# Order of the first feed-forward chunk in a fused attention and SwiGLU kernel

## The chip, the cores and the metric

The kernel runs on one core of a Trainium2 chip. The metric is the device time of one execution in microseconds (us), given as the median of five runs. One more view of the kernel is a profile of one execution, in which every instruction of every engine has a start and a length. The engines are named as the profile names them: PE is TensorE's matmul, PEld its weight load, DVE is VectorE, ACT is ScalarE, POOL is GpSimd and SP is SyncE.

## The reference, cut to what matters

Eight batches of eight heads, 576 positions, 64 numbers per head; 32 memory slots. The result of the attention is a matrix of 4608 rows and 512 columns, which goes through a gated feed-forward layer:

```python
a = softmax(phi, axis=2)                       # over the sequence
k_m = einsum('bhsm,bhsd->bhmd', a, k)
v_m = einsum('bhsm,bhsd->bhmd', a, v)
attn = softmax(scale * q @ k_m.T)              # over the 32 memory slots
x = (attn @ v_m)                               # heads side by side: 512 columns
g = x @ w_gate
out = (g * sigmoid(g) * (x @ w_val)) @ w_out   # 512 -> 1536 -> 512
```

## The kernel before, in words

The kernel never forms x. For each batch it multiplies the small matrix v_m (256 rows in all: 8 heads by 32 slots) with the gate and value weights; the products are called U. Gate and value of the layer are then the attention weights A times U. Both are cut into chunks of 512 of the 1536 columns (`NCH` is 3), and a chunk into two halves of 256.

A round of U (`u_round`, line 453) is a set of matmuls `p_u` on TensorE (line 465) into PSUM banks, and then one copy per bank into the SBUF tile `t_U`. Each round for one weight and one half is eight matmuls of 256 columns into two banks, each for half of the heads. A string tells who makes the copies, one letter a bank: "a" is ACT (line 487), "v" is DVE (line 491). In batches 0 and 1 the copy also multiplies by the reciprocal of the softmax's sum. Gate weights are `which` 0, value weights 1. `u_half(b, which, c, half, evac)` is a round of one half of chunk `c`; with `which` (0, 1) it puts gate and value side by side into the same two banks, so that there are 16 matmuls and two copies of 512 columns. `u_item(b, c)` is gate and value of a whole chunk, with four copies.

After it come the slots. A slot is one block of 128 hidden columns by 288 positions; a batch has 24, eight a chunk, and slots 0 to 3 of a chunk use its first half. `gv_gate(b, s)` (line 517) makes two matmuls `p_g` (A times U of the gate, line 508) and a silu on ACT (line 525), and puts the rest on the list `pend`: two matmuls `p_v` with the value half of U and a product on DVE (line 531) into `t_h`. `flush_mul(n)` carries out the first n of the list. `gv_slot` is `gv_gate` and then what was pending before it, so that p_v and the product run one slot behind.

All is ordered by hand: the program's order is the order on each engine's queue, and an engine waits where its next instruction's data are not there. Every matmul group takes the next of eight PSUM banks in turn, in the order of their release in the program (`bank` and `done`, lines 75 to 84). A group therefore waits for the reader of the bank that was taken eight groups earlier.

The weights come by DMA, issued on POOL's queue (`load_w`, line 128). For chunk 0 they come in halves, in the order gate half 0, value half 0, gate half 1, value half 1, after k, q and v of batches 0 and 1; then chunks 1 and 2 whole, then w_out and the inputs of the next batches.

Before the stretch that is changed, attention of batches 0 and 1 is done: `v_direct(1)` makes v_m of batch 1, with its four DVE copies to `t_kT`, and `norm(1, 1)` (line 445) is the last normalization, a DVE product that follows an Exp on ACT (line 421). Softmax uses ACT's table of Ln and Exp; silu needs another table, loaded by `preload_act_table_set`. `warm` (line 868) is matmuls of no result that keep TensorE occupied.

After the stretch, from chunk 1 on, rounds and slots of both batches alternate to the end of chunk 2; then come the output products (line 720) and batches 2 to 7.

Of the kernel before, what the change touches and what calls it, by code (L numbers as in the profile page):

```python
# [14 lines left out]
def kernel(  # L15
# [427 lines left out]
    def norm(b, g):  # L443
        a = att.tile([128, 2, HALF], BF16, tag=f"A{g}", name="t_A")
        nc.vector.tensor_tensor(out=a, in0=es.pop((b, g)), in1=lzs.pop((b, g)), op=ALU.mult)  # L445
        atts[b, g] = a
# [6 lines left out]
    def u_round(b, parts, evac):  # L453


        banks = []
        for which, c, halves in parts:
            w0, w1, h0, h1 = which[0], which[-1] + 1, halves[0], halves[-1] + 1
            n = (h1 - h0) * HC
            p = [bank([128, CH], FP32, f"p_u{g}") for g in range(NG)]  # L460
            for w in which:
                o = (w - w0) * n
                for i in range(NP):
                    for g in range(NG):
                        nc.tensor.matmul(  # L465
                            p[g][32 * i:32 * i + 32, o:o + n],
                            lhsT=kTs[b][64 * g:64 * g + 64, 2, 32 * i:32 * i + 32],
                            rhs=w_part(w, c, i, g, halves),
                            start=True,
                            stop=True,  # L470
                            tile_position=(64 * g, 32 * i),
                        )
            for g in range(NG):
                if (b, c, g) not in Us:
                    u_buffer(b, c, f"U{c}")
                if len(which) == 1:
                    dst = Us[b, c, g][:, h0:h1, w0]
                else:
                    dst = Us[b, c, g][:, h0]
                src = p[g][:, 0:(w1 - w0) * n].rearrange("p (a f) -> p a f", f=HC)  # L480
                banks.append((dst, src, p[g], rSs[b][:, g:g + 1] if b in scaled else None))
        for (t, p, home, r), e in zip(banks, evac):
            if e == "a":
                if r is None:
                    nc.scalar.copy(out=t, in_=p)  # L485
                else:
                    nc.scalar.activation(out=t, in_=p, func=AF.Copy, scale=r)  # L487
            elif r is None:
                nc.vector.tensor_copy(out=t, in_=p)  # L489
            else:  # L490
                nc.vector.tensor_scalar(out=t, in0=p, scalar1=r, scalar2=None, op0=ALU.mult)
            done(home)
# [5 lines left out]
    def flush_mul(n=None):  # L498
        for _ in range(len(pend) if n is None else n):
            pend.pop(0)()  # L500
# [16 lines left out]
    def gv_gate(b, s):  # L517

        jf, r = s // 2, s % 2
        c, o = jf // 4, jf % 4  # L520
        if o == 0 and r == 0:
            hts[b, c] = hpool.tile([128, 4, S], BF16, tag=f"h{c}", name="t_h")
        gate = gv_half(b, s, 0)
        sg = work.tile([128, HALF], BF16, tag="sg", bufs=8, name="t_sg")
        nc.scalar.activation(out=sg, in_=gate[:, 0:HALF], func=AF.Silu)  # L525
        done(gate)
        dst = hts[b, c][:, o, r * HALF:(r + 1) * HALF]

        def mul():
            val = gv_half(b, s, 1)  # L530
            nc.vector.tensor_tensor(out=dst, in0=sg, in1=val[:, 0:HALF], op=ALU.mult)  # L531
            done(val)
            if o == 3 and r == 1:
                chunk_done(b, c)

        pend.append(mul)
# [288 lines left out]
    def u_item(b, c, evac="avav"):  # L825

        return lambda: u_round(b, (((0,), c, (0, 1)), ((1,), c, (0, 1))), evac)

    def u_half(b, which, c, half, evac):

        return lambda: u_round(b, ((which, c, (half,)),), evac)
# [9 lines left out]
    def run(items):  # L841
        for x in items:
            x()
# [13 lines left out]
    def gv_slots(b):  # L857
        return [lambda s=s: gv_slot(b, s) for s in range(2 * NJF)]
# [84 lines left out]


    g0, g1 = gv_slots(0), gv_slots(1)
    run([u_half(0, (0,), 0, 0, "av")])
    nc.scalar.preload_act_table_set("silu_and_others")
    norm(1, 1)
    run([u_half(1, (0,), 0, 0, "vv")])
    for s in range(4):  # L950
        gv_gate(0, s)
    run([u_half(0, (1,), 0, 0, "vv"), u_half(1, (1,), 0, 0, "aa")])
    for s in range(2):
        gv_gate(1, s)
    flush_mul(3)
    run([u_half(0, (0, 1), 0, 1, "va"), u_half(1, (0, 1), 0, 1, "av")])
    flush_mul(2)
    run(g1[2:4] + g0[4:8] + g1[4:5])
    for c in range(1, NCH):
        s = 8 * c  # L960
        run([u_item(0, c)] + g1[s - 3:s] + g0[s:s + 5])
        run([u_item(1, c)] + g0[s + 5:s + 8] + g1[s:s + 5])
    run(g1[-3:])
    flush_mul()
# [146 lines left out]
```

The softmax here doesn't subtract the row's maximum and nothing guards it: scores larger than these inputs give would overflow.

## Time and profile before

| | us |
|---|---|
| Median of five runs | 234.18 |
| Lowest and highest | 234.13 and 234.78 |
| The profiled execution, its own time | 234.78 |
| Span of the profile (first to last instruction) | 233.0 |
| End of the last Exp of the softmax of batches 0 and 1 (ACT) | 24.94 |
| End of the last copy to t_kT (DVE) | 25.89 |
| First round of U starts on TensorE | 25.93 |
| u_item(0, 1) starts | 34.86 |
| u_item(1, 1), u_item(0, 2), u_item(1, 2) start | 39.44, 44.03, 48.61 |
| First output product starts | 54.81 |

All times in the profile are counted from the start of the span. The profiled execution is one of the five, and the slowest of them. The next section shows lines of the profile. A line of the timeline gives start, length, engine, source line, operation, what is written and what is read, and how many instructions are merged into it; in brackets stands the idle time before it and what ended it. The chain of waits is read in order of time: at each step it names the work that the next step had to wait for.

### The profile page before, as it was taken

How to read it: one execution, taken by the hardware profiler on the slowest of the kernel's cores; microseconds unless marked ns; L12 is line 12 of the kernel's file. 1: busy time of each engine (PE TensorE's matmuls, PEld its weight loads, DVE VectorE, ACT ScalarE, POOL GpSimd, SP SyncE). 2: the span in 40 equal slices, each digit the busy share in tenths (PEclk: the TensorE clock that was granted, in tenths of full speed). 3: DMA queues.
4: the chain of work that ended last, by engine and by line, in shares of the span. 5: the costliest groups of instructions: out<-in, count | busy, mean ns of one | idle time of the engine just before them, and what ended most of it. 6: DMA issues, size and time to landing. Idle time of an engine off the chain costs nothing.

```text
span 233.0 us, 7208 instructions
## 1 busy us (share of the span) xinstructions
PE 222.6 (96%) x2825; PEld 169.6 (73%) x2825; DVE 186.3 (80%) x426; ACT 171.2 (73%) x364; POOL 140.6 (60%) x190
## 2 busy tenths in 40 slices
PE   7977899999999999999999999999999999999993
PEld 2544466778887777877788777887788778878882
DVE  4245799999966799989997758998999899977732
ACT  2777798988447989968896658987898789677310
POOL 8422426998099049765977688553945394029291
PEclk9999999999999999999999999999999999999999
DMA  6999999999995992999199994996022702202125
GB/s 210 209 211 206 199 207 207 227 239 268 205 247 129 265 253 47 224 207 188 52 219 197 182 177 90 252 238 109 3 90 92 125 0 94 85 7 90 24 92 159
DMA packets 36674, 36.84 MB, mean 158 GB/s; under 512 B 14624, under 2 KB 31008, under 8 KB 36640
## 3 DMA queue, kind: packets, MB, share of 16 engines
q0 software_dynamic: 16272, 22.42, 52.1%
q1 hardware_dynamic: 19600, 13.18, 23.3%
q10 hardware_dynamic: 768, 0.79, 1.1%
q8 instruction: 22, 0.36, 0.6%
q14 instruction: 12, 0.10, 0.1%
HBM read 42.47 MB, written 9.44 MB: 223 GB/s over the span
## 4 chain that ended last, share of the span: by engine, by line
PE 88%; DMA 7%; POOL 1%; ACT 1%; issue 1%; DVE 1%; POOLq 0%
PE p_g L508 21%; PE p_os L720 21%; PE p_v L508 20%; PE p_oc L720 10%; DMA t_kv<-in_v_dram 7%; PE p_u L465 5%; PE p_oa L720 5%; PE p_kv L230 2%; PE p_g L389 1%; POOL t_kv L99 1%; PE p_mT L318 1%; PE p_warm L868 1%; PE p_q L376 0%; POOL t_q L108 0%; DVE t_kT L332 0%
## 5 line engine op out<-in xcount | busy, mean ns | idle before, releaser
L531 DVE TENSOR_TENSOR t_h<-t_sg,p_v 128x288 bf16<-128x288 bf16 x192 | 81.5, 452 | 14.0 <-PE p_v L508 7.8
L508 PEld LDWEIGHTS <-t_U 128*128 128x128 bf16 x768 | 73.6, 98 | 22.3 <-issue 3.3
L525 ACT ACTIVATE t_sg<-p_g 128x288 bf16<-128x288 f32 x192 | 73.9, 423 | 17.8 <-PE p_g L508 11.5
L508 PE MATMUL p_g<-t_A,t_U 128*128 128x288 bf16 x384 | 77.1, 286 | 0.5 <-ACT t_U L487 0.5
L508 PE MATMUL p_v<-t_A,t_U 128*128 128x288 bf16 x384 | 76.9, 286 | 0.0
L720 PEld LDWEIGHTS <-t_S 128*128 128x128 bf16 x384 | 37.5, 98 | 4.6 <-issue 0.2
L596 POOL TENSOR_TENSOR t_S<-t_h 128x512 bf16<-128x512 bf16 x17 | 19.7, 1156 | 34.3 <-DVE t_h L531 32.2
L720 PEld LDWEIGHTS <-t_h 128*128 128x128 bf16 x288 | 27.1, 98 | 8.6 <-issue 5.0
L485 ACT CAST t_U<-p_u 128x512 bf16<-128x512 f32 x51 | 27.0, 607 | 6.6 <-PE p_u L465 6.6
L720 PE MATMUL p_os<-t_T,t_S 128*128 128x256 bf16 x192 | 23.7, 273 | 0.0
L553 POOL TENSOR_TENSOR t_S<-t_S,t_h 128x512 bf16<-128x512 bf16 x17 | 19.6, 1155 | 1.3
L553 POOL TENSOR_TENSOR t_S<-t_h,t_S 128x512 bf16<-128x512 bf16 x16 | 18.4, 1153 | 0.0
L553 POOL TENSOR_TENSOR t_S<-t_h 128x512 bf16<-128x512 bf16 x16 | 18.4, 1151 | 0.0
L465 PE MATMUL p_u<-W,t_kT 64*32 64x512 bf16 (+1 forms) x416 | 15.8, 364 | 0.6 <-DVE t_kT L332 0.6
L489 DVE CAST t_U<-p_u 128x512 bf16<-128x512 f32 x21 | 13.6, 684 | 1.9 <-PE p_u L465 1.9
L720 PE MATMUL p_os<-t_T,t_h 128*128 128x256 bf16 x96 | 14.8, 273 | 0.0
L868 PE MATMUL p_warm<-bones 128*128 128x512 bf16 x44 | 12.5, 422 | 1.7 <-DVE bones L890 1.7
L445 DVE TENSOR_TENSOR t_A<-t_E,t_lz 128x576 bf16<-128x576 bf16 x16 | 11.4, 740 | 0.7 <-ACT t_lz L421 0.7
L720 PE MATMUL p_oc<-t_T,t_S 128*128 128x256 bf16 x96 | 12.0, 273 | 0.0
L720 PE MATMUL p_oa<-WO,t_h 128*128 128x256 bf16 x96 | 11.8, 273 | 0.0
L720 PE MATMUL p_oc<-WO,t_S 128*128 128x256 bf16 x96 | 11.8, 272 | 0.1
L720 PE MATMUL p_os<-WO,t_h 128*128 128x256 bf16 x96 | 11.8, 273 | 0.0
(106 smaller groups left out, 308.9 us busy)
## 6 DMA issues: line engine op xcount, KB each, us to landing
out_dram<-t_o SPq DMA_DIRECT2D x11, 512.0 KB, 3.0
t_kv<-in_k_dram POOLq DMA_DIRECT2D x8, 576.0 KB, 10.7
t_q<-in_q_dram POOLq DMA_DIRECT2D x8, 576.0 KB, 9.0
t_kv<-in_v_dram POOLq DMA_DIRECT2D x8, 576.0 KB, 15.4
t_phi<-in_phi_dram POOLq DMA_DIRECT2D x6, 576.0 KB, 8.6
out_dram<-t_o SPq DMA_DIRECT2D x10, 256.0 KB, 3.5
WO<-in_moe_w_out_dram POOLq DMA_DIRECT2D x3, 512.0 KB, 19.2
W<-in_moe_w_gate_dram POOLq DMA_DIRECT2D x2, 512.0 KB, 16.4
```

The source lines that it names most:

```text
L230: nc.tensor.matmul(p[g][32 * i:32 * i + 32, 0:n], lhsT=phi_of(b, g, j, i), rhs=kvs[b][64 * g:64 * g + 64, w0:w1, i, j * D:(j + 1) * D], st ...
L445: nc.vector.tensor_tensor(out=a, in0=es.pop((b, g)), in1=lzs.pop((b, g)), op=ALU.mult)
L465: nc.tensor.matmul(p[g][32 * i:32 * i + 32, o:o + n], lhsT=kTs[b][64 * g:64 * g + 64, 2, 32 * i:32 * i + 32], rhs=w_part(w, c, i, g, halve ...
L485: nc.scalar.copy(out=t, in_=p)
L489: nc.vector.tensor_copy(out=t, in_=p)
L508: nc.tensor.matmul(p[:, 0:HALF], lhsT=Us[b, c, g][:, o // 2, which, 128 * (o % 2):128 * (o % 2 + 1)], rhs=atts[b, g][:, r], start=(g == 0) ...
L525: nc.scalar.activation(out=sg, in_=gate[:, 0:HALF], func=AF.Silu)
L531: nc.vector.tensor_tensor(out=dst, in0=sg, in1=val[:, 0:HALF], op=ALU.mult)
L553: eng.tensor_tensor(out=out, in0=x, in1=y, op=ALU.subtract)
L596: eng.tensor_tensor(out=t[:, 0], in0=A21, in1=A22, op=ALU.add)
L720: nc.tensor.matmul(mine[home][:, u], lhsT=lhs(c, m, u), rhs=rhs(c, m), start=fresh and u == 0, stop=(k == 5), skip_group_check=u == 1 or n ...
L868: nc.tensor.matmul(p[:, 0:128 * a], lhsT=bones, rhs=x.to_broadcast([128, a, 128]) if a > 1 else bones, start=True, stop=True,)
```

## The change

It reorders the first chunk of batches 0 and 1. The load of silu's table moves ahead of the first round. The gate half of batch 0, then its value half, then gate and value of batch 1 (side by side, two wide copies) follow one another before any slot; formerly the value halves of both came after the first four slots of batch 0. Copies that were all DVE's or all ACT's are shared by the two. Pending products are flushed in another rhythm: two after the first four slots, then one after each slot of batch 1, and none is left over after the second half's rounds. The second half's copies for batch 1 are both ACT's. One slot more of batch 1 (`g1[4:6]`) stands before `u_item(0, 1)`, and one fewer after it.

```diff
     g0, g1 = gv_slots(0), gv_slots(1)
-    run([u_half(0, (0,), 0, 0, "av")])
     nc.scalar.preload_act_table_set("silu_and_others")
+    run([u_half(0, (0,), 0, 0, "va")])
     norm(1, 1)
-    run([u_half(1, (0,), 0, 0, "vv")])
+    run([u_half(0, (1,), 0, 0, "va"), u_half(1, (0, 1), 0, 0, "av")])
     for s in range(4):
         gv_gate(0, s)
-    run([u_half(0, (1,), 0, 0, "vv"), u_half(1, (1,), 0, 0, "aa")])
+    flush_mul(2)
     for s in range(2):
         gv_gate(1, s)
-    flush_mul(3)
-    run([u_half(0, (0, 1), 0, 1, "va"), u_half(1, (0, 1), 0, 1, "av")])
+        flush_mul(1)
+    run([u_half(0, (0, 1), 0, 1, "va"), u_half(1, (0, 1), 0, 1, "aa")])
     flush_mul(2)
-    run(g1[2:4] + g0[4:8] + g1[4:5])
+    run(g1[2:4] + g0[4:8] + g1[4:6])
     for c in range(1, NCH):
         s = 8 * c
-        run([u_item(0, c)] + g1[s - 3:s] + g0[s:s + 5])
+        run([u_item(0, c)] + g1[s - (2 if c == 1 else 3):s] + g0[s:s + 5])
         run([u_item(1, c)] + g0[s + 5:s + 8] + g1[s:s + 5])
```

## The prediction

> **What bounds the kernel now.** I read the page from the top, then the chain of waits, then the timeline of the stretch that the diff touches. Shares first:
>
> ```profile
> PE 222.6 (96%) x2825; PEld 169.6 (73%) x2825; DVE 186.3 (80%) x426; ACT 171.2 (73%) x364; POOL 140.6 (60%) x190
> ...
> PEclk9999999999999999999999999999999999999999
> ...
> PE 88%; DMA 7%; POOL 1%; ACT 1%; issue 1%; DVE 1%; POOLq 0%
> ```
>
> TensorE holds 88% of the chain at its full clock, so the kernel is bound by TensorE, and only what shortens TensorE's own queue counts. The 7% of DMA lie before 21.2 us, where the inputs arrive. The diff works between 25.9 and 35 us. There the chain of waits reads (start, length, what; x9 means nine instructions):
>
> ```profile
> 25.96 0.37 PE p_u L465 x9
> 26.33 0.47 ACT t_U L487
> ...
> 26.85 1.16 PE p_g L508 x8
> 28.01 0.32 PE p_u L465 x9
> ...
> 28.35 0.30 PE p_u L465 x7
> 28.65 0.63 PE p_g L508 x4
> 29.28 0.85 PE p_v L508 x6
> 30.13 0.78 PE p_u L465 x32
> 30.91 0.60 PE p_v L508 x4
> 31.50 0.24 PE p_g L508 x2
> ```
>
> The reader should see that TensorE is on the chain throughout but not dense. From 31.5 us on, each pair of p_g or p_v matmuls takes 0.245 us, that is 0.1224 each. Before that, one ACT copy stands in the chain, four p_g matmuls take 0.63 in place of 0.49, six p_v take 0.85 in place of 0.73, and a round of sixteen p_u is cut in two at 28.35. The timeline says what the other engines did meanwhile:
>
> ```profile
> 26.82 1.28 ACT L947 ACT_TABLE_LOAD   x1
> ...
> 27.42 1.76 DVE L491 TENSOR_SCALAR t_U<-p_u,t_rS 128x256 bf16<-128x256 f32 x4
> ...
> 28.11 1.32 ACT L525 ACTIVATE t_sg<-p_g 128x288 bf16<-128x288 f32 x4
> 28.35 0.11 PEld L465 LDWEIGHTS <-t_kT 64*32 64x32 bf16 x6 [0.29 <-issue]
> ...
> 30.50 0.14 PEld L465 LDWEIGHTS <-t_kT 64*32 64x32 bf16 x14 [0.21 <-issue]
> 30.58 1.33 ACT L487 ACTIVATE t_U<-p_u,t_rS 128x512 bf16<-128x512 f32 x2
> ```
>
> ACT loads its table for 1.28 us in the middle of this, so DVE has to make four copies in a row. "issue" names no releaser, but the order of the banks does: there are eight, used in turn, so a group of matmuls needs the reader of the bank eight places earlier to be done. At 28.35 that is the second of the four DVE copies (27.42 + 2 x 0.44 = 28.30), at 30.50 the first silu of batch 1. Last, the weights. The DMA issues, each with its time from issue to landing, of a window around 6.7 us:
>
> ```profile
> W<-in_moe_w_gate_dram POOLq DMA_DIRECT2D x1, 256.0 KB, 19.8
> W<-in_moe_w_val_dram POOLq DMA_DIRECT2D x1, 256.0 KB, 20.1
> ```
>
> POOL issued them at 6.01 and 6.74 (timeline), so the first half of the gate weights landed at 25.81 and that of the value weights at 26.84. Nothing waits for the latter now: its round starts at 27.94.
>
> **What the Trainium skill says.** "ScalarE: Activation LUTs", section "What ACT_TABLE_LOAD costs", gives 1283 ns for the load and 1380 ns of drain. The trace agrees on the load (1.28) and shows no drain: the silu starts at 28.11, 0.01 after it. I take 1.28. "TensorE: Matmul & The Clock Gate", section "Why this matters for your kernels", warns of idle gaps over some 3 us, after which the clock falls. The longest gap here is 1.28 us, before 18.29, with the clock full; the gap I expect below is shorter. "DMA: Bandwidth & Descriptors", section "Two DMAs through the same engine are not ordered", says that the completion semaphore is what tells that data has landed: a value round may not start on the strength of the gate half's landing. Its first matmul carries such a wait.
>
> **The change part by part.** The matmuls, the copied elements and the queues of POOL and SP stay as they are. Of the copies, eight narrow (256 columns) and four wide (512) become four narrow and six wide, otherwise shared between ACT and DVE; TensorE's queue is reordered.
>
> *Table load.* It moves to directly behind the last Exp of the normalization, which ends at 24.94, so it runs to 26.22. The first p_u is ready at 26.32. It is covered, with 0.1 us to spare. Without that cover it would cost up to 1.28.
>
> *First gate round and its two copies.* The engines change places; both took 0.47 to 0.48. Nothing.
>
> *Rounds in a row.* Now TensorE has 8 gate, 8 value (batch 0), then 16 (batch 1) p_u matmuls before any p_g. What goes:
> - the wait of the first p_g for the ACT copy, 26.33 to 26.85: 0.52;
> - the bank wait at 28.35: 0.29, as batch 1's round no longer reuses banks of copies just queued on DVE (it takes banks that were read before 25);
> - p_v waiting for the last of the four DVE copies (27.42 + 1.76 = 29.18): 0.63 - 0.49 = 0.14;
> - the bank wait at 30.50: 0.21. The silus of batch 1 now come before the wide copies are wanted: by my count they end at about 29.9 and 30.3, and their banks are next used after 30.5;
> - two changes between p_u and p_g/p_v fewer (five become three). One costs about 0.12: the six p_v above, 0.85 - 0.73. Together 0.24.
>
> Sum of what goes: 1.40.
>
> What comes in its place: the value round stands second in TensorE's queue. The first round starts at 25.93 and has issued its eight by about 26.05 (0.12, an estimate from 16 matmuls of 0.28 that all end within 0.41). Value weights land at 26.84; with 0.04 from landing to start (the v of batch 0: landing 21.13, weight load 21.17) it starts at 26.88. New wait: 0.83. Behind it on TensorE are batch 1's rounds, whose weights are there, and all p_g; behind those, every silu.
>
> From there by hand: 24 p_u and a change of kind bring the first p_g to about 27.35. Ten pairs (four p_g, two p_v, then p_g and p_v twice) of 0.245 bring the second half's rounds to 29.9, against 30.06 before and with one p_v pair more done. The copies keep up: DVE does norm 26.67 to 27.42, a copy of 0.44, then a wide one of 0.70, done at 28.5, and batch 1's first p_g wants it at 28.8. ACT does a narrow copy from 27.2, a wide one, and starts silu at 28.25, 0.14 later than before; the first bank that needs it is wanted at 29.3.
>
> *Second half, "aa".* ACT now has three wide copies of 0.62 to 0.64 in a row from about 30.45, done at 32.35, with the silus of slots 2 and 3 behind them; DVE gets one, and idles. TensorE has seven pairs to do from 30.5, so it wants the last of these banks at 32.2 (gate of slot 5 of batch 0). It waits 0.1; bounds 0 and 0.3, since each start above can be 0.1 off.
>
> *One slot more before the next round.* That round needs value weights that land at 34.53 (issue 18.53, 16.0 to landing); it moves one slot (0.49) back and comes at about 34.9, as before, so there is no wait. The work is the same from the following round on.
>
> Sum: 1.40 - 0.83 - 0.10 = 0.47 us gained, at the hand-over to the next stage (54.7 us before). What could swallow it there is far enough: v of batch 2 lands at 54.35 for matmuls at 59.04, q of batch 2 at 58.54 for 59.77. POOL's sums start behind the same p_v as before and move along. So I carry 0.47 to the end: the profiled execution would take 234.31 instead of 234.78 (its span 232.5 instead of 233.0). The median of the five runs lies 0.60 under that execution, and I take the gain off the median: **233.71, rounded to 233.7**.
>
> **Rivals.**
> - *The value weights are there in time* (233.3). If the landing is not what holds the round, for instance because the runs without a profile fetch faster, the new wait shrinks to that for the first p_g's copies (26.8, about 0.4 of 0.83 saved): gain about 0.85. For it: the profiled execution is the slowest of five by 0.6. Against: batch 1's v, which starts the stretch, comes through the same queue just before, and would be earlier too.
> - *No change* (234.2). ACT's three copies cost the upper 0.3 and the changes of kind bring nothing; or TensorE meets a transfer later, since landings do not move with it. For it: ACT's margin is about nothing. Against: the slacks just given.
> - *Slower* (234.7), by one mechanism: the value weights land later than in this trace. The whole of TensorE's queue stands behind that round, including batch 0's p_g, which needed only gate weights before. Every 0.1 us later costs 0.1; it decides from 27.3 on (26.84 + 0.47) and is slower by over 0.2% from about 27.8. For it: POOL's next issue that waits for this landing ran only at 27.34. Against: that issue also waits for other semaphores, and the others of its kind follow their landings by 0.31.
>
> **How the numbers follow.** Forecast 0.60, weights in time 0.13, no change 0.13, slower 0.14. A measurement of this kernel tells some 0.2%, or 0.47 us, from no change; the forecast sits on that edge. I count 0.7 of its chance beyond it, because where I rounded (the changes of kind, the bank waits) TensorE can as well gain 0.1 more. Faster: 0.42 + 0.13 = 0.55. Same: 0.18 + 0.13 = 0.31. Slower: 0.14. The forecast's own range is 233.45 to 233.95, from the bounds of the ACT wait and 0.15 on the sum of gaps. The range 233.25 to 234.35 takes in the first two rivals and leaves out the last.
>
> **What would show it.** In the profile after: a table load at about 24.95; a TensorE gap of about 0.8 before the second round, with the W DMA as releaser and its start at 26.9; the first p_g at about 27.35; no split at the later rounds; a gap of 0 to 0.3 near 32.3 behind ACT's third copy; the round of chunk 1 at about 34.9 and those after it some 0.5 earlier than 39.4, 44.0 and 48.6. It is wrong if the second round starts before 26.6 or after 27.2, if ACT's copies hold TensorE by over 0.3, or if the lead at 54 us is not there at the end.

## The result, and the profile after

The change makes the kernel a little faster: 233.55 us in the median of 24 runs (233.30 to 234.15), against 234.15 for the kernel before (44 runs). The ratio is 0.9977, 95% interval 0.9972 to 0.9983, that is 0.54 us less (0.40 to 0.66); the two medians alone lie 0.60 apart. The prediction was 233.7, range 233.25 to 234.35. The profiled execution of after took 233.9 us, its span is 232.1.

The page of after, shares of the engines, TensorE's clock, and the chain by engine:

```profile
PE 223.2 (96%) x2825; PEld 170.0 (73%) x2825; DVE 185.3 (80%) x423; ACT 171.6 (74%) x365; POOL 140.6 (61%) x190
...
PEclk9999999999999999999999999999999999999999
...
PE 86%; DMA 9%; POOL 2%; ACT 1%; issue 0%; DVE 0%; POOLq 0%
```

TensorE still bounds the kernel. But DMA's share of the chain has grown from 7 to 9%, and it is another transfer: before, the chain came out of the DMAs at 21.2 us, with v of batch 0; now it comes out at 26.9, with the value weights. A part of this step is only how the first profile of before was read: in a second profile of before the chain comes out of the gate weights, at 25.64, and DMA has 8%. The chain of waits of after, in order of time (start, length, what):

```profile
6.74 20.16 DMA W<-in_moe_w_val_dram
26.91 0.04 issue
26.95 0.52 PE p_u L465 x24
27.47 1.09 PE p_g L508 x8
28.55 0.49 PE p_v L508 x4
29.05 0.24 PE p_g L508 x2
...
30.03 0.56 PE p_u L465 x32
30.59 0.60 PE p_v L508 x4
31.18 0.49 PE p_g L508 x4
...
32.16 0.24 PE p_v L508 x2
32.41 0.35 PE p_g L508 x2
32.76 0.24 PE p_v L508 x2
```

From the landing at 26.90 on, TensorE is dense: p_v and p_g take 0.245 a pair, and the rounds of 24 and 32 are no longer cut. A group that follows a round takes 0.11 more than its pairs (1.09 for eight, 0.60 for four). Beyond that there is one blemish, the pair at 32.41, which stands for 0.35 where 0.245 is due. Who makes what when, from the timeline of after:

```profile
25.27 1.28 ACT L946 ACT_TABLE_LOAD   x1
...
25.78 0.30 PE L465 MATMUL p_u<-W,t_kT 64*32 64x256 bf16 x8
...
26.24 0.48 DVE L491 TENSOR_SCALAR t_U<-p_u,t_rS 128x256 bf16<-128x256 f32 x1
26.57 0.47 ACT L487 ACTIVATE t_U<-p_u,t_rS 128x256 bf16<-128x256 f32 x1
...
26.95 0.52 PE L465 MATMUL p_u<-W,t_kT 64*32 64x256 bf16 x24 [0.86 <-DMA W<-in_moe_w_val_dram]
...
30.46 1.84 ACT L487 ACTIVATE t_U<-p_u,t_rS 128x512 bf16<-128x512 f32 x3 [0.24 <-PE p_u L465]
```

The bracket names the new wait outright. Note the two copies of the first round: DVE starts at 26.24, ACT only at 26.57, right behind the table load, which in this execution ended at 26.55.

For the comparison of runs three times of the timeline do most of the work: the start of the first round, the start of the second (value) round, and the first output product, where the stage ends. Of before and of after there is a second profile, of another execution.

| kernel, one execution each | first round | value round | stage's end | stage's end less first round | stage's end less value round |
|---|---|---|---|---|---|
| before | 25.96 | 27.94 | 54.81 | 28.85 | |
| before, second profile | 25.77 | 27.74 | 54.62 | 28.85 | |
| after | 25.78 | 26.95 | 54.36 | 28.58 | 27.41 |
| after, second profile | 25.88 | 26.65 | 54.06 | 28.18 | 27.41 |

The ends of the stage, in the order of the table, and ahead of the last one the second round of that profile:

```profile
54.81 1.47 PE L720 MATMUL p_os<-WO,t_h 128*128 128x256 bf16 x12
...
54.62 1.47 PE L720 MATMUL p_os<-WO,t_h 128*128 128x256 bf16 x12
...
54.36 1.47 PE L720 MATMUL p_os<-WO,t_h 128*128 128x256 bf16 x12
...
26.65 0.52 PE L465 MATMUL p_u<-W,t_kT 64*32 64x256 bf16 x24 [0.47 <-DMA W<-in_moe_w_val_dram]
...
54.06 1.47 PE L720 MATMUL p_os<-WO,t_h 128*128 128x256 bf16 x12
```

So the kernel before takes 28.85 us from its first round, and the kernel after 27.41 from its second. What the change gains is 28.85 - 27.41 = 1.44, less the distance between the two rounds: 1.17 in the first profile of after, 0.77 in the second. That leaves 0.27 and 0.67. (The ends themselves differ by 0.45 and 0.56, because the first rounds do not start at the same time either.) The distance is set by two DMA landings and differs from execution to execution. Three of the experiments below leave these two rounds as they are in after; in their profiles it is 0.99 (late table load), 1.15 (shared copies) and 0.89 (one slot less). The mean of the five is 0.99, with which the formula gives a gain of 0.45, against 0.54 measured.

The spans differ by 0.9, twice the 0.45 by which the stages' ends differ. The other 0.46 come from a stall in batch 4, told below.

### The profile page after: what moved, and what is told of

The parts are those of the page before. It is cut to its first block, busy times and chain, and to the rows that moved or that the text cites. A ratio compares the mean times of both kernels' runs of the same rounds, so it can differ in the third digit from the quotient of the medians.

```text
span 232.1 us, 7206 instructions
## 1 busy us (share of the span) xinstructions
PE 223.2 (96%) x2825; PEld 170.0 (73%) x2825; DVE 185.3 (80%) x423; ACT 171.6 (74%) x365; POOL 140.6 (61%) x190
## 4 chain that ended last, share of the span: by engine, by line
PE 86%; DMA 9%; POOL 2%; ACT 1%; issue 0%; DVE 0%; POOLq 0%
PE p_g L508 21%; PE p_os L720 21%; PE p_v L508 20%; PE p_oc L720 10%; DMA W<-in_moe_w_val_dram 9%; PE p_oa L720 5%; PE p_u L465 5%; PE p_kv L230 2%; PE p_g L389 1%; POOL t_kv L99 1%; POOL t_kv L103 1%; PE p_q L376 0%; POOL t_q L108 0%; ACT t_qT L330 0%; POOL W L138 0%
## 5 line engine op out<-in xcount | busy, mean ns | idle before, releaser
L465 PE MATMUL p_u<-W,t_kT 64*32 64x512 bf16 (+1 forms) x416 | 15.3, 363 | 0.9 <-DMA W<-in_moe_w_val_dram 0.9
L868 PE MATMUL p_warm<-bones 128*128 128x512 bf16 x44 | 13.9, 459 | 1.7 <-DVE bones L890 1.7
```

What stands on the lines that cost most here:

```text
L465: nc.tensor.matmul(p[g][32 * i:32 * i + 32, o:o + n], lhsT=kTs[b][64 * g:64 * g + 64, 2, 32 * i:32 * i + 32], rhs=w_part(w, c, i, g, halve ...
L868: nc.tensor.matmul(p[:, 0:128 * a], lhsT=bones, rhs=x.to_broadcast([128, a, 128]) if a > 1 else bones, start=True, stop=True,)
```

## The experiments

Ratios are against the kernel before, run beside it.

**The table load put back behind the first round.**

```diff
-    nc.scalar.preload_act_table_set("silu_and_others")
     run([u_half(0, (0,), 0, 0, "va")])
+    nc.scalar.preload_act_table_set("silu_and_others")
     norm(1, 1)
```

> The kernel after with the table load behind the first round's copies again. Theory (the load was covered only because it lies before the first round; behind it, it delays ACT's copies and silus, and TensorE waits for banks and for the value copies): the whole gain goes, 234.1, within 0.15 of the kernel before; in the profile p_v of slot 0 waits for the ACT copy. Rival (the wait for the value weights, 26.1 to 26.9, hides most of the load wherever it is put): at most 0.2 above the kernel after, 233.75.

Measured: 234.17, ratio 0.9998 (0.9990 to 1.0006). The gain is gone, as the theory had it. ACT's lines in the timeline:

```profile
26.21 0.47 ACT L487 ACTIVATE t_U<-p_u,t_rS 128x256 bf16<-128x256 f32 x1 [1.09 <-PE p_u L465]
26.70 1.28 ACT L947 ACT_TABLE_LOAD   x1
28.00 1.05 ACT L487 ACTIVATE t_U<-p_u,t_rS 128x256 bf16<-128x256 f32 x2
28.94 1.91 ACT L525 ACTIVATE t_sg<-p_g 128x288 bf16<-128x288 f32 x6
```

The copy of the value round starts at 28.00 in place of 27.34 and the silus at 28.94 in place of 28.29. From the value round (26.80) to the stage's end (54.69) it takes 27.89, 0.48 more than after. TensorE's lines show where:

```profile
28.25 0.82 PE L508 MATMUL p_v<-t_A,t_U 128*128 128x288 bf16 x4
29.11 0.42 PE L508 MATMUL p_g<-t_A,t_U 128*128 128x288 bf16 x2
...
30.19 0.74 PE L465 MATMUL p_u<-W,t_kT 64*32 64x256 bf16 x32
```

p_v of slot 0 waits for that copy, and the p_g behind it for ACT's next one: from the first p_v to that p_g it is 0.86 (28.25 to 29.11) in place of 0.49 in after (28.39 to 28.88). The round of 32 then takes 0.74 in place of 0.63. Together these are the 0.48; from there on the two profiles run alike. The wait for the value weights does not hide a table load that comes after the first copy, since ACT is needed again as soon as that wait ends.

**The early table load alone, in the kernel before.**

```diff
-    run([u_half(0, (0,), 0, 0, "av")])
     nc.scalar.preload_act_table_set("silu_and_others")
+    run([u_half(0, (0,), 0, 0, "av")])
     norm(1, 1)
```

> The kernel before with nothing but the early table load. Theory (the waits of the kernel before are for copies of the rounds in their old places: the first ACT copy, four DVE copies in a row; only the wait at 30.5 goes, and another bank takes its place): no gain, 234.1, between -0.2 and +0.1 of the kernel before. Rival (the table load in the middle is what cost the time, the order of the rounds is immaterial): the gain of the whole change, 233.55.

Measured: 234.21, ratio 0.9998 (0.9989 to 1.0006): nothing. In its profile the stage takes 28.72 from the first round (25.87 to 54.59), 0.13 less than before. TensorE still waits 0.48 for the first ACT copy and meets the same four DVE copies. The wait at 30.5 is gone, as expected, and pairs further on come late instead (0.28, 0.29 and 0.36 after the one ahead of them at 31.45, 32.47 and 32.83, where 0.245 is due). So neither the early load alone nor the rest of the change without it gives the gain. The rest itself (the rounds in a row, who makes which copy, the rhythm of the flushes) was not taken apart further, but for the "aa" and the extra slot below.

**The second half's copies of batch 1 shared ("av") in the kernel after.**

```diff
-    run([u_half(0, (0, 1), 0, 1, "va"), u_half(1, (0, 1), 0, 1, "aa")])
+    run([u_half(0, (0, 1), 0, 1, "va"), u_half(1, (0, 1), 0, 1, "av")])
```

> The kernel after with the second half's copies for batch 1 shared (one ACT, one DVE) and not both on ACT. Theory (ACT's third copy holds TensorE by 0.1 near 32.3): 0.1 faster than the kernel after, 233.45, and the gap before the gate of slot 5 is gone. Rival (both on ACT frees DVE for the products, and the shared form moves the wait to a product on DVE): 0.1 to 0.3 slower than the kernel after.

Measured: 233.76, ratio 0.9978 (0.9968 to 0.9988), in time not to be told from after's 0.9977. The profile can tell it: from the value round (26.93) to the stage's end (54.23) 27.30, 0.11 less than after's 27.41, and the pair behind 31.98 follows at 32.23, without a gap. At the stage's end the theory's 0.1 is there and the rival's loss is not; the times alone could not exclude a small loss.

**The value weights later.** Both gate halves first, then both value halves; in the kernel after, and as a control in the kernel before.

```diff
-    for half in range(2):
-        for which in range(2):
+    for which in range(2):
+        for half in range(2):
             load_w(which, 0, half)
```

> The kernel after with the weights of chunk 0 fetched in another order: both gate halves, then both value halves, so that the first value half lands third, by about 28.2 in place of 26.9. Theory (TensorE's whole queue stands behind the second round, every 0.1 us later costs 0.1): 1.2 to 1.3 slower than the kernel after, 234.8, with TensorE idle from about 26.1 to 28.2. Rival (the round is not bound by this landing, or the copies and slots behind it have slack that takes up a part): at most 0.6 slower than the kernel after, 234.1.

> The kernel before with the weights of chunk 0 in the order of e4: the first value half lands by about 28.2. Theory (in the kernel before, the value rounds start only at 27.94 and their second half waits for a bank until 28.35 anyway): 0 to 0.3 slower than the kernel before, 234.3, with the clock full, so that the loss of e4 is that of the moved round. Rival (the other order of the weights costs by itself, for instance through the later loads): 1 or more slower, as in e4.

Measured on after: 236.78, but spread: 234.84 and 234.90 in two of seven runs, 236.48 to 237.73 in the others; ratio 1.0092 (1.0060 to 1.0123). The two low runs are the 1.3 of the theory. The others lost about 2 more, which neither theory nor rival had. Each run also has a mean granted clock: 0.996 and 0.997 in the two low ones, as in undisturbed runs of the other kernels, and 0.985 to 0.993 in the five others. The profiled run is one of these five (236.48). The windows of its profile show where the clock was lost (columns: window, length, then busy time and number of instructions of PE, PEld, DVE, ACT and POOL, then the granted clock of TensorE, DMA share, GB/s):

```profile
26.00:27.00 1.00, 0.30 (x8) 0.14 (x9) 0.53 (x2) 0.65 (x2) 0.74 (x1) 1.00 1.45 196
27.00:28.00 1.00, 0.00 (x0) 0.00 (x0) 0.62 (x1) 0.00 (x0) 0.74 (x1) 0.84 1.44 199
28.00:29.00 1.00, 0.87 (x25) 0.44 (x25) 0.39 (x1) 0.36 (x1) 0.63 (x1) 0.50 1.28 207
29.00:30.00 1.00, 1.00 (x5) 0.62 (x6) 0.82 (x2) 1.00 (x3) 0.16 (x2) 0.50 1.24 206
30.00:31.00 1.00, 1.00 (x6) 0.59 (x4) 0.00 (x0) 0.84 (x3) 0.71 (x1) 0.50 1.26 208
31.00:32.00 1.00, 1.00 (x10) 0.78 (x8) 0.53 (x2) 0.53 (x2) 0.00 (x0) 0.95 1.22 203
```

The clock falls to half between 27 and 28 (the mean of 0.84 puts it at about 27.7) and stays there until about 31.1. 3.4 us at half clock are 0.7% of the span, which fits the run's mean of 0.993. On TensorE's timeline of the same profile:

```profile
26.11 0.30 PE L465 MATMUL p_u<-W,t_kT 64*32 64x256 bf16 x8 [0.77 <-DMA W<-in_moe_w_gate_dram]
28.13 0.84 PE L465 MATMUL p_u<-W,t_kT 64*32 64x256 bf16 x24 [1.72 <-DMA W<-in_moe_w_val_dram]
28.91 2.10 PE L508 MATMUL p_g<-t_A,t_U 128*128 128x288 bf16 x8
```

Eight p_g take 2.10 in place of 1.16. From the value round to the stage's end (56.92) it is 28.79, 1.38 more than in after. What came before is an idle stretch from 25.34 to 28.13 with only 0.30 of work in it; the clock fell before that stretch was over.

Measured on before: 234.45, ratio 1.0016 (1.0006 to 1.0025), so 0.37 slower (0.14 to 0.59) where 0 to 0.3 was expected; TensorE waits 0.50 for the weights at 28.50, with its clock full. So the new order of the weights costs little by itself; the loss on after is that of the round that was moved forward.

**The same with TensorE kept busy:** matmuls of no result between the rounds, on top of the later value weights.

```diff
+    warm(32)
     run([u_half(0, (1,), 0, 0, "va"), u_half(1, (0, 1), 0, 0, "av")])
```

> e4 with eight matmuls of no result (512 columns each, 1.7 us in all) between the first and the second round, so that TensorE does not idle while it waits for the value weights. Theory (e4 lost 1.3 by the later landing and the rest because TensorE's clock fell to half after the idle stretch): the clock stays full and the time is 1.3 above the kernel after, 234.9, in all runs. Rival (the other 2 us of e4 come from something else, for instance DMA): 236.8 as e4, spread as wide.

Measured: 235.29 (234.82 to 235.34, five runs), ratio 1.0047 (1.0033 to 1.0062). The spread and the other loss are gone, and the clock is full in all windows of the profiled stretch. TensorE's timeline:

```profile
26.23 1.90 PE L868 MATMUL p_warm<-bones 128*128 128x512 bf16 x8
28.19 0.52 PE L465 MATMUL p_u<-W,t_kT 64*32 64x256 bf16 x24
28.64 1.15 PE L508 MATMUL p_g<-t_A,t_U 128*128 128x288 bf16 x8
```

From the value round (28.19) to the stage's end (55.60) it is 27.41, exactly after's. The time is 0.4 above the expected 234.9: the round starts 1.24 and 1.54 later than in the two profiles of after, and in the profiled execution the stretch of batch 4 told below took 0.35 more than its shortest. The filler may have held the round by some 0.1 itself: its weight load is at 28.06, its first matmul at 28.19.

**Two slots ahead of the value round,** to give TensorE work during the wait.

```diff
+    for s in range(2):
+        gv_gate(0, s)
     run([u_half(0, (1,), 0, 0, "va"), u_half(1, (0, 1), 0, 0, "av")])
-    for s in range(4):
+    for s in range(2, 4):
         gv_gate(0, s)
```

> The kernel after with slots 0 and 1 of batch 0 (their p_g and silus) ahead of the value rounds, so that TensorE has work while the value weights come in. Theory (p_g starts at 26.8 when the copies are done; the value rounds and their copies come 0.5 later, and the p_g of batch 1 then waits for them by 0.1 to 0.2): the wait for the weights goes from 0.86 to the wait for the copies, 0.6, and the end is about the same as the kernel after, 233.55 to 233.75. Rival (the wait for the weights is lost time in full, and work put there is gained in full): 0.5 faster, 233.1.

Measured: 233.83, ratio 0.9996 (0.9986 to 1.0005): not to be told from before, and slower than the theory's upper end. One of the 21 runs took 235.72, at a mean granted clock of 0.989 (the other twenty are at 0.997 or more), so the clock seems to have fallen in it as in the experiment above; without it the mean lies 0.2 below before, still 0.3 short of after. The rival, for which the wait is time that can be had back in full, falls. TensorE's timeline says what was missed:

```profile
25.83 0.30 PE L465 MATMUL p_u<-W,t_kT 64*32 64x256 bf16 x8
26.77 0.91 PE L508 MATMUL p_g<-t_A,t_U 128*128 128x288 bf16 x4 [0.64 <-DVE t_U L491]
27.62 0.52 PE L465 MATMUL p_u<-W,t_kT 64*32 64x256 bf16 x24
```

The first p_g waits for DVE's copy, the second for ACT's, which cannot start before the table load ends (26.60 here). The two waits are 0.64 and some 0.24 (the four p_g take 0.91, where four behind a round take 0.67 elsewhere), and p_g of batch 1 waits some 0.13 more for its own copy, as the theory had said. Together that is 1.0, more than the 0.86 it replaced in after, where the two copies lie under the wait for the weights.

**Batch 0 ahead of v of batch 1.** The first halves of the weights are fetched before v of batch 1, and batch 0's rounds and four slots take the place of filler matmuls. The copies of the second half are shared ("av") here, too.

```diff
+    for which in range(2):
+        load_w(which, 0, 0)
     load_v(1)
...
-    norm(1, 0)
-    warm(16)
-    v_direct(1, "vvvv")
-    warm(8)
...
-    run([u_half(0, (0,), 0, 0, "va")])
+    run([u_half(0, (0,), 0, 0, "vv")])
+    warm(8)
+    run([u_half(0, (1,), 0, 0, "vv")])
+    norm(1, 0)
     norm(1, 1)
...
     flush_mul(2)
+    v_direct(1, "vava")
+    flush_mul(2)
+    run([u_half(1, (0, 1), 0, 0, "av")])
...
```

> A version meant to be faster than both: the first gate and value halves are fetched before v of batch 1, and batch 0's rounds, copies (all on DVE) and first four slots are done on TensorE before v of batch 1 arrives; the filler matmuls there go. Theory (TensorE's time between 23 and 26 us holds no needed work now but filler, as it waits for v of batch 1; batch 0's rounds and slots need only its own v): 0.4 to 1.0 faster than the kernel after, 232.8. Rival (v of batch 1 lands 2 x 1.2 us later, and its round then holds up the rest; or the idle stretch lowers the clock): no gain or slower, 233.6 to 235.

Measured: 233.92, ratio 0.9997 (0.9989 to 1.0005). The rival was right in time, and in the first of its two reasons: what batch 0 gained, batch 1 lost. The clock stayed full. TensorE:

```profile
26.81 0.76 PE L318 MATMUL p_mT<-t_mphi,t_kv 128*64 128x64 bf16 x36 [0.88 <-DMA t_kv<-in_v_dram]
...
29.81 0.66 PE L508 MATMUL p_g<-t_A,t_U 128*128 128x288 bf16 x4 [0.79 <-ACT t_U L487]
```

First it waits for v of batch 1, then for a copy of batch 1's round.

**One slot less before the round of chunk 1,** in the kernel after.

```diff
-    run(g1[2:4] + g0[4:8] + g1[4:6])
+    run(g1[2:4] + g0[4:8] + g1[4:5])
...
-        run([u_item(0, c)] + g1[s - (2 if c == 1 else 3):s] + g0[s:s + 5])
+        run([u_item(0, c)] + g1[s - 3:s] + g0[s:s + 5])
```

> The kernel after without the extra slot before the round of chunk 1 (that slot comes after it again). Theory (the value weights of chunk 1 land at about 34.3 to 34.5, and the round, 0.49 earlier, would want its second half at about 34.5): nothing or up to 0.2 slower than the kernel after. Rival (the slot of distance is needed, as ACT and DVE are still behind): 0.3 or more slower.

Measured: 233.75, ratio 0.9985 (0.9977 to 0.9992), whose interval overlaps that of after, so the times don't tell the two apart. In the profile that round takes 0.70 in place of 0.62, and value round to stage's end is 27.49, 0.08 more than after. The weight load of the round's second half waits 0.18 for the value weights there. The extra slot is worth about that 0.08, by this one profile.

**Second profiles of before and after, for batch 4.** Both kernels unchanged, one execution each.

> The kernel before once more, for one stretch of batch 4, from one table load to the next: 22.81 us in the profile of before, 22.35 in that of after, without a releaser for the difference. Theory (a stall of that execution, not of the program): another length, between 22.1 and 22.8. Rival (the program of before always has it): 22.7 to 22.8 again.

> The kernel after once more. Theory: the stretch of batch 4 is of another length than 22.35, between 22.1 and 22.8, and the first stage repeats: a wait of 0.7 to 0.9 for the value weights and the round of chunk 1 some 8.0 after the second round's start. Rival: 22.35 again, the same in every execution of this program.

In the first profile of before, the chain of waits has one line in batch 4 without a releaser:

```profile
136.21 0.11 PE p_oc L720
136.31 0.51 issue
136.82 0.60 PE p_oc L720 x4
```

At the same matmul after has 0.05. Between the two table loads around it lie 22.81 us in the first profile of before, 22.14 in the second, 22.35 and 22.20 in the two of after. So the stall comes and goes with the execution, and before does not always have it. Over all profiles, the stretch is long (22.81, and 22.74 in the experiment with the early table load) in two of four with the order of before, and 22.14 to 22.49 in all nine with the order of after and its variants. That is too few to say that the change has no part in it: the means differ by 0.2, and that much of the measured gain, or nothing, may come from there. What the stall is stays open.

The second profile of after repeats the first stage, but with a wait of 0.47 for the value weights, less than the 0.7 to 0.9 that had been expected; the round of chunk 1 starts 7.95 after the second round in both. In the second pair the stages' ends differ by 0.56 and the times by 0.45 (233.93 and 233.48).

## Why the prediction was right

It expected 0.47 us less; 0.54 (0.40 to 0.66) were measured. The mechanism is the one it named: waits for copies go, and a wait for the value weights takes back a good half of them. Term by term:

- *The waits that go.* Expected 1.40 in five terms, of which the bank waits and the wait of p_v are seen to be gone in the chain of after. Two terms were read off each other's lines. The four p_g of 0.63 follow a round, and after shows what that costs: 0.11. The six p_v of 0.85 follow p_g, where after shows no extra (0.49 for four), so their 0.12 is the wait for DVE's copies and not a change of kind. The sizes are nearly equal, so the sum hardly suffers; that is luck. What the runs confirm is the sum: 1.44 from the stage's lengths, which also holds the first round's own 0.12 and the 0.1 lost to ACT. By the prediction's own terms that is 1.40 + 0.12 - 0.10 = 1.42.
- *The new wait.* Expected 0.83, at 26.88; measured 0.86, at 26.95, and 0.47, at 26.65, in the second profile (0.69, 0.85 and 0.59 in the three experiments with the same two rounds). So the one trace of before gave nearly the upper end of a range. The experiments with the later weights give its price: 1.24 later costs 1.24 at the stage's end (55.60 against 54.36) while the clock stays full.
- *What starts the first round was told wrongly.* The prediction let v of batch 1 start the stretch, and used that against the first rival. The first round needs only batch 0's v_m, whose copies were done at 22.96; in after it starts at 25.78, when the copies of batch 1 still run (to 26.20). What it waits for is the gate weights: in all four profiles it starts some 0.15 after they land (issue plus time to landing, for instance 25.77 after a landing at 25.6 in the second profile of before, which names this DMA as the releaser). So the distance of the rounds is that of two weight landings, and the first rival (weights in time) and the forecast are the ends of one scale. The second profile of after stands between them, with 0.67 gained by the formula above, and the mean of five profiles, 0.45, at the forecast.
- *The table load.* It was expected at 24.94 and to be covered with 0.1 to spare. In the first profile it started at 25.27, and ACT's first copy came 0.33 behind DVE's. That cost nothing because TensorE was waiting for the weights; the two-slots experiment shows the cost once that cover is gone. In the second profile it started at 24.91, and ACT's copy came 0.04 behind. "Up to 1.28" without cover was a bound: behind the first copy the load cost 0.48 at the stage's end.
- *ACT's three copies.* Expected 0.1 near 32.3, between 0 and 0.3; measured 0.11 at 32.36 (0.36 from one pair to the next in place of 0.245), and 0.11 less without them.
- *The extra slot.* Right: the round of chunk 1 started at 34.90, and without the slot it lost 0.08.
- *The lead is kept.* After is 0.46 ahead of before at the table load of 54.5 us and 0.45 at that of 122.3 (first profiles): the later stages move as a block.
- *The slower rival* had the price right, as the run with filler shows, but left out the clock: with the weights 1.2 later its fall costs as much again, and it came in five of seven runs. The prediction had dismissed the clock, as the gap it expected was shorter than one that did no harm; for that gap this was right. How late the weights may land before the clock falls was not measured.

## What to carry to other kernels

Price a reordering by the wait that ends last in the new order: here 1.4 us of waits for copies went, and 0.5 to 0.9 of it came back as a wait for a transfer that nobody had waited for. Look up its landing time before moving a consumer forward, in more than one execution: here it moved the gain between 0.27 and 0.67. A piece of work that is hidden (the table load, ACT's late copy) is hidden by a certain wait, and costs its price as soon as something fills that wait.

## What the runs showed of the hardware

With the value weights later, TensorE's clock fell to half at about 27.7 us. TensorE had last been steadily at work at 25.34, 2.3 us before; in between eight small matmuls ran for 0.30 us, and the longest gap of the stretch, 1.72 us, was not yet over. The clock stayed at half for some 3.4 us, which cost 1.38 us at the end of the stage. It happened in five of seven runs by their mean clock; what decides in which is open. With filler matmuls of 1.90 us in that stretch it did not happen in any of five. "TensorE: Matmul & The Clock Gate" of the Trainium skill, section "Why this matters for your kernels", warns of gaps over some 3 us between bursts; here the clock fell with no gap that long, so a short burst in between did not help. A single gap of 1.28 us in the kernel before and one of 0.86 us in the kernel after left it full.

Four copies from one bank to one tile, given in turn to DVE and ACT in the experiment with batch 0 ahead, waited for one another: they started at 27.61, 27.86, 28.10 and 28.36, each after the first with the one before it as its releaser, and took 0.96 us in all, no faster than four in a row on DVE (0.98). Whether the shared bank or the shared tile makes them wait was not tested.
